# Later float32r copies in MLP 1's last block, and another low-word shift in MLP 2's weight conversions

## The chip, the cores and the metric

The kernel runs on one core of a Trainium2 chip. The metric is the device time of one execution in microseconds; lower is better. The kernel before takes 602.6 us (median of 3 runs, 602.4 to 602.93). Engines are called by their short names in the rows: PE is TensorE (PEld its weight loads), DVE VectorE, ACT ScalarE, POOL GpSimd, SP SyncE, whose queue issues most DMAs.

## The reference

The inputs pass through a blocked linear attention and two MLPs, each of 1536 tokens by 512 features with 2048 hidden features:

```python
x = attn(q, k, v, lam)                    # 2 batches, 8 heads, 768 tokens, 64 features a head
h = x @ w1_in                             # MLP 1
x = (h * np.clip(h + 3, 0, 6) / 6) @ w1_out
h = x @ w2_in                             # MLP 2
P = a[0] + a[1]*h + a[2]*h**2 + a[3]*h**3
Q = 1 + abs(b[0])*abs(h) + abs(b[1])*h**2
out = (P / (Q + 1e-6)) @ w2_out
```

The weights arrive as 64-bit floats. The kernel reads them as pairs of 32-bit words and makes each float32 value on the chip.

## The kernel before

**Tiling.** Tokens go in three blocks of 512, hidden features in 16 tiles of 128. One step `s` is one token block with one feature tile: steps 0 to 47 are MLP 1, steps 48 to 95 MLP 2. Each step has a first product `mm1(s)` (12 matmuls into `hb[s % 2]`, one of two PSUM banks), an activation, and a second product `mm2(s)` (12 matmuls into the four `acc` banks). Each operand is split into a high and a low float32r part, so a product takes three matmuls. `mm2` runs two to three steps behind `mm1`; the list `turns` fixes the order of the two on TensorE.

**Order.** The body runs under a manual schedule: every engine carries out its instructions in the order in which the program writes them, and waits by semaphores for the others. Tiles from a pool with `bufs=2` alternate between two buffers.

**Activation of MLP 2** (`act2`, lines 283 to 297, and `act2_rest`, 301 to 306). ScalarE writes |b0 h| into the PSUM bank `X` (L289), then h squared into `ta` (L290), `tb` (L291), `tc` (L292) and `td` (L293); L293 is the last reader of `hb`. VectorE adds `X` to `tb` (L294). GpSimd multiplies and adds (L295, L296). One step later in the program VectorE takes the reciprocal into the PSUM bank `Y` (L304) and multiplies (L305). `act_fin` then makes the high part `gh` on ScalarE (L280) and the low part `gl` on GpSimd (L281), which `mm2` reads.

**Weight conversion.** A job is one or two tiles of weights, loaded as raw 64-bit words. `conv_c` copies the scaled high words (ACT L153) and clamps them (DVE L154). `conv_l` or `conv_s` shifts them by three bits and brings in the top bits of the low words; `conv_l` uses a PSUM bank for that (X or Y), `conv_s` the raw tile. `conv_w` puts the sign in (DVE L194). `conv_h` makes the float32r copy on ScalarE (L207) and the low part on GpSimd (L208). In MLP 1's last block (steps 32 to 47) each step converts one tile of MLP 2's input weights and one of its output weights. The last three output tiles are converted in MLP 2: the list `later` holds their pieces, and each step from 52 on takes one piece off it, between `act_fin(s - 2)` and `mm1(s)` in program order.

**The places that the diff touches.** `pending` holds copies (`conv_h`) that are made in the next step, right behind that step's activation; before, only output weights go there. `late` selects, in `conv_s`, a form on VectorE alone (L181 and L184).

Of the kernel before, what the change touches and what calls it, by code (L numbers as in the profile page):

```python
# [10 lines left out]
U32 = mybir.dt.uint32  # L11
BF16 = mybir.dt.bfloat16
AF = mybir.ActivationFunctionType
ALU = mybir.AluOpType
# [16 lines left out]
def fused_kernel(  # L31
# [14 lines left out]
    nc = tc.nc  # L46
# [4 lines left out]
    KD = DM // 128  # L51
# [18 lines left out]
    X = ps.tile([128, 512], F32, name="X")  # L70
    Y = ps.tile([128, 512], F32, name="Y")
# [27 lines left out]
    jobs = [[(0, 0)], [(0, 1)]] + [[(0, f + 2)] * (f < NF - 2) + [(1, f)] for f in range(NF)]  # L99
    NJ1 = len(jobs)  # L100
    jobs += [[(2, p)] * (p < NF) + [(3, p - LAG)] * (p >= LAG) for p in range(NF + LAG)]
    N1 = NB * NF
# [5 lines left out]
    for s in range(NSTEP):  # L108
# [5 lines left out]
        while at < to:  # L114
            d, i = quarters[at]
# [3 lines left out]
    while at < len(quarters) - 8:  # L119
        d, i = quarters[at]  # L120
# [4 lines left out]
    def load_job(j):  # L125
        if j >= len(jobs):
            return
        t = []
        for m, f in jobs[j]:
            r = rp.tile([128, KD, 128, 2], U32, name=f"raw{m % 2}")  # L130
            if m % 2 == 0:
                nc.sync.dma_start(
                    r.rearrange("p k f t -> p k (f t)"),
                    w32[m].rearrange("(k p) f -> p k f", p=128)[:, :, 256 * f : 256 * f + 256],
                )
            else:
                nc.sync.dma_start(r.rearrange("p k f t -> p (k f t)"), w32[m][128 * f : 128 * f + 128, :])
            t.append(r)
        raw[j] = t

    conv = {}
# [12 lines left out]
        nc.vector.tensor_scalar(out=x, in0=x, scalar1=CMAX, scalar2=-CMAX, op0=ALU.min, op1=ALU.max)  # L154
        conv[j, i] = x

    def conv_l(j, i):

        if i >= len(jobs[j]):
            return  # L160
        x = conv[j, i]
        y = (X, Y)[i].bitcast(U32).rearrange("p (a b) -> p a b", a=KD)
        nc.scalar.activation(y, raw[j][i][:, :, :, 0], AF.Copy, scale=LOWS, bias=LOWB)
        nc.vector.scalar_tensor_tensor(  # L164
            out=y, in0=x.bitcast(U32), scalar=3, in1=y, op0=ALU.logical_shift_left, op1=ALU.bitwise_or
        )
        conv[j, i] = x, y, x.bitcast(U32)

    def conv_s(j, i, late=False):

        if i >= len(jobs[j]):
            return
        x = conv[j, i]
        y, r = x.bitcast(U32), raw[j][i]
        if not late:
            nc.scalar.activation(r[:, :, :, 0], r[:, :, :, 0], AF.Copy, scale=LOWS, bias=LOWB)
            nc.vector.scalar_tensor_tensor(
                out=y, in0=y, scalar=3, in1=r[:, :, :, 0], op0=ALU.logical_shift_left, op1=ALU.bitwise_or
            )
        else:  # L180
            nc.vector.tensor_scalar(  # L181
                out=y, in0=y, scalar1=3, scalar2=1, op0=ALU.logical_shift_left, op1=ALU.bitwise_or
            )
            nc.vector.scalar_tensor_tensor(  # L184
                out=y, in0=r[:, :, :, 0], scalar=29, in1=y, op0=ALU.logical_shift_right, op1=ALU.bitwise_or
            )
        conv[j, i] = x, y, r[:, :, :, 1]

    def conv_w(j, i):
# [21 lines left out]
    def mm1(s):  # L211
        tb, f = (s // NF) % NB, s % NF
        ih, il = W["in", f]
        h = hb[s % 2]
        for kk in range(KD):
            nc.tensor.matmul(h, lhsT=ih[:, kk, :], rhs=xh[tb][:, kk, :], start=kk == 0, stop=False)  # L216
        for kk in range(KD):
            nc.tensor.matmul(h, lhsT=il[:, kk, :], rhs=xh[tb][:, kk, :], start=False, stop=False)  # L218
        for kk in range(KD):
            nc.tensor.matmul(h, lhsT=ih[:, kk, :], rhs=xl[tb][:, kk, :], start=False, stop=kk == KD - 1)  # L220

    def mm2(s, ds=(0, 1, 2, 3)):
        tb, f = (s // NF) % NB, s % NF
        oh, ol = W["out", f]
        gh, gl = g_t[s]
        first = s < NB * NF
        st, sp = f == 0, f == NF - 1
        for d in ds:
            c = slice(128 * d, 128 * d + 128)
            if first:  # L230
                ops = ((oh[:, c], gh), (ol[:, c], gh), (oh[:, c], gl))
            else:
                ops = ((gh[:, c], oh), (gh[:, c], ol), (gl[:, c], oh))
            for i, (l, r) in enumerate(ops):
                nc.tensor.matmul(acc[d], lhsT=l, rhs=r, start=st and i == 0, stop=sp and i == 2)  # L235
            if sp:
                if first:
                    nc.scalar.activation(xh[tb][:, d, :], acc[d], AF.Copy, scale=1.0 / 6.0)
                    nc.vector.scalar_tensor_tensor(
                        out=xl[tb][:, d, :], in0=acc[d], scalar=1.0 / 6.0,  # L240
                        in1=xh[tb][:, d, :].bitcast(F32), op0=ALU.mult, op1=ALU.subtract,
                    )
                else:
                    o = rp.tile([128, KD, 128, 2], U32, name=f"raw{d % 2}").bitcast(F32)
                    o = o.rearrange("p k f t -> p (k f t)")[:, 0:DM]
                    row = TB * tb + 128 * d
                    if s == NSTEP - 1 and d == 3:
                        for e, eng, dma in ((0, nc.scalar.copy, nc.scalar), (1, nc.vector.tensor_copy, nc.sync)):
                            hf = slice(DM // 2 * e, DM // 2 * e + DM // 2)
                            eng(o[:, hf], acc[d][:, hf])  # L250
                            dma.dma_start(out[row : row + 128, hf], o[:, hf])
                    else:
                        nc.scalar.copy(o, acc[d])  # L253
                        nc.sync.dma_start(out[row : row + 128, :], o)
# [54 lines left out]
    with ExitStack() as actx:  # L309
# [106 lines left out]
        with tc.manual_schedule():  # L416
# [18 lines left out]
            for h2 in range(2):  # L435
                r = slice(64 * h2, 64 * h2 + 64)
                nc.vector.tensor_copy(lamq[r, :], lamb.rearrange("p (a b) -> p a b", b=2)[r, :, h2])
            for p in range(NP):
                nc.vector.tensor_tensor_scan(
                    out=qtab[:, p, :], data0=lamq[:, p : p + 1].to_broadcast([128, CH]), data1=zero,  # L440
                    initial=1.0, op0=ALU.mult, op1=ALU.add)
                for h2 in range(2):
                    hd = 2 * p + h2
                    nc.vector.tensor_tensor_scan(
                        out=dmat[:, h2, p, :], data0=lamb[:, hd : hd + 1].to_broadcast([128, CH]), data1=ident,
# [23 lines left out]
            att_t(2, hb)  # L469
            conv_all(conv_c, 0)  # L470
            conv_all(conv_s, 0)
            conv_all(conv_w, 0)
            att_o(1)
# [35 lines left out]
            for s in range(att_steps):  # L509
                c = CPT + s  # L510
                j = s + 3
# [41 lines left out]
    W2AT = N1 - NF  # L553
    with tc.manual_schedule():
        pending, later = [], []
        nc.scalar.activation(b1a, b_sb[:, 1:2], AF.Abs)
        todo = turns[turns.index((1, att_steps + 1)) :]
        for at, (kind, s, *qs) in enumerate(todo):
            if kind == 2:
                mm2(s, *qs)  # L560
                continue
            j = None
            if s + 2 < NJ1:
                j = s + 2
            elif s >= W2AT and s - W2AT + NJ1 < len(jobs):
                j = s - W2AT + NJ1
            if s == W2AT - 1:
                load_job(NJ1)
            if j is not None and j != NJ1 - 1:
                load_job(j + 1)  # L570
            n = 0 if j is None else len(jobs[j])
            if s < N1:
                mm1(s)
                act1(s)
                if todo[at + 1][0] == 2 and todo[at + 1][1] % NF == NF - 1:
                    act_fin(s)
                    mm2(*todo.pop(at + 1)[1:])
                for p in pending:
                    conv_h(*p)
                if n:  # L580
                    conv_c(j, 0)
                    conv_l(j, 0)
                    conv_w(j, 0)
                act_fin(s)
                if s == N1 - 1:

                    later += [(conv_c, j, 1, True), (conv_s, j, 1, True), (conv_w, j, 1), (conv_h, j, 1)]
                    n = 1
                if n > 1:
                    conv_c(j, 1)  # L590
                    conv_l(j, 1)
                    conv_w(j, 1)
            else:
                act2_rest(s - 1)
                act_fin(s - 2)
                if s > N1 + LAG2 and later:
                    f, *args = later.pop(0)
                    f(*args)
                mm1(s)
                act2(s)  # L600
                for p in pending:
                    conv_h(*p)
                if n:
                    later += [(conv_c, j, 0, True), (conv_s, j, 0, True), (conv_w, j, 0), (conv_h, j, 0)]
                n = 0
            pending = []
            for i in range(n):
                if jobs[j][i][0] % 2:
                    pending.append((j, i))
                else:  # L610
                    conv_h(j, i)
            if s == NSTEP - 1:
                act2_rest(s)
                act_fin(s - 1)
                act_fin(s)
# [29 lines left out]
```

## Time and profile before

| what | value |
|---|---|
| median of 3 runs | 602.6 us |
| profiled execution | 602.82 us |
| span of the profiled execution, first to last instruction | 600.9 us |
| TensorE busy | 588.1 us (98%) |
| VectorE busy | 445.2 us (74%) |
| ScalarE busy | 384.0 us (64%) |
| GpSimd busy | 366.8 us (61%) |
| granted TensorE clock | 1.00 of full speed |

Times within the profile count from the first instruction. The 1.9 us between the profiled execution's time and its span lie around the program's own instructions. Busy shares are averages over the whole span and don't tell which engine the others wait for in a given stretch.

### The profile page before, as it was taken

Reading aid. Unit: us, or ns where it says so; the run is one execution under the profiler, and the core shown is the slowest. Engines: PE = TensorE matmul, PEld = TensorE weight load, DVE = VectorE, ACT = ScalarE, POOL = GpSimd, SP = SyncE. Lnnn points to the kernel's source line nnn. Section 1 sums busy time; section 2 is a strip of 40 time slices with the busy share of each in tenths; the row PEclk is TensorE's granted clock in tenths of the full one; section 3 lists DMA queues with packets and bytes.
Section 4 is the critical chain, followed back from the end, with each engine's and each line's share of the span. In section 5 each row is a group of like instructions: output and inputs, shape, how many; then the busy total and the mean of one; then the engine's idle time right before and its main releaser. Section 6 shows DMA issues by size and latency. Waiting matters only on the chain.

```text
span 600.9 us, 8288 instructions
## 1 busy us (share of the span) xinstructions
PE 588.1 (98%) x3035; PEld 480.6 (80%) x3035; DVE 445.2 (74%) x476; ACT 384.0 (64%) x635; POOL 366.8 (61%) x291
## 2 busy tenths in 40 slices
PE   8898999999999999999999999999999999999997
PEld 5786888888888888888888787877788888888886
DVE  5877888787411011488888899999999888999991
ACT  2566465677422222588787877787887767877771
POOL 3756677566421222266676677688776677777772
PEclk9999999999999999999999999999999999999999
DMA  8987755364000000266655000000010000100001
GB/s 169 267 214 196 173 157 160 130 211 150 1 1 0 1 0 1 88 206 197 184 171 172 1 1 35 1 0 2 28 43 0 2 0 2 69 2 0 1 1 71
DMA packets 61289, 46.68 MB, mean 78 GB/s; under 512 B 39104, under 2 KB 55744, under 8 KB 61248
## 3 DMA queue, kind: packets, MB, share of 16 engines
q1 hardware_dynamic: 60960, 46.02, 26.9%
q8 instruction: 24, 0.39, 0.3%
q10 hardware_dynamic: 288, 0.14, 0.1%
q14 instruction: 17, 0.14, 0.1%
HBM read 43.00 MB, written 3.15 MB: 77 GB/s over the span
## 4 chain that ended last, share of the span: by engine, by line
PE 52%; DVE 24%; ACT 4%; issue 3%; POOL 1%; DVEq 0%; ACTq 0%
PE acc L235 26%; DVE Y L304 8%; PE hb L216 8%; PE hb L220 8%; PE hb L218 8%; DVE ta L154 2%; DVE X L164 2%; DVE ta L194 2%; DVE Y L164 2%; DVE tb L294 2%; DVE tb L194 2%; ACT ta L153 1%; DVE td L305 1%; DVE tb L154 1%; DVE raw L184 1%
## 5 line engine op out<-in xcount | busy, mean ns | idle before, releaser
L304 DVE RECIPROCAL Y<-tb 128x512 f32<-128x512 f32 x48 | 161.3, 3360 | 1.6
L281 POOL TENSOR_TENSOR gl<-td,gh 128x512 fp32r<-128x512 f32 x84 | 111.2, 1324 | 77.1 <-ACT gh L280 76.0
L216 PE MATMUL hb<-xh,wih 128*128 128x512 f32 x384 | 104.3, 393 | 0.5 <-ACT td L293 0.4
L218 PE MATMUL hb<-xh,wil 128*128 128x512 f32 x384 | 102.7, 389 | 0.0
L220 PE MATMUL hb<-xl,wih 128*128 128x512 f32 x384 | 102.6, 389 | 0.0
L295 POOL TENSOR_TENSOR tc<-ta,tc 128x512 f32<-128x512 f32 x48 | 62.2, 1295 | 58.2 <-ACT tc L292 58.2
L271 DVE SCALAR_TENSOR_TENSOR td<-tc,hb 128x512 f32<-128x512 f32 x48 | 32.8, 683 | 84.3 <-ACT tc L268 84.3
L216 PEld LDWEIGHTS hb<-xh,wih 128*128 128x128 f32 x384 | 71.1, 188 | 17.4 <-ACT td L293 1.8
L218 PEld LDWEIGHTS hb<-xh,wil 128*128 128x128 f32 x384 | 72.1, 188 | 15.2
L220 PEld LDWEIGHTS hb<-xl,wih 128*128 128x128 f32 x384 | 72.1, 188 | 15.0
L268 ACT ACTIVATE tc<-hb,c 128x512 f32<-128x512 f32 x48 | 32.9, 686 | 71.7 <-PE hb L220 71.6
L235 PE MATMUL acc<-gh,woh 128*128 128x512 f32 x192 | 76.1, 396 | 0.0
L235 PE MATMUL acc<-gl,woh 128*128 128x512 f32 x192 | 74.8, 390 | 0.0
L235 PE MATMUL acc<-gh,wol 128*128 128x512 f32 x192 | 74.8, 389 | 0.0
L280 ACT CAST gh<-td 128x512 fp32r<-128x512 f32 x84 | 52.0, 619 | 25.9 <-DVE td L271 13.8
L296 POOL TENSOR_TENSOR td<-td,tc 128x512 f32<-128x512 f32 x48 | 63.8, 1330 | 3.8
L208 POOL TENSOR_TENSOR wil<-ta,wih 128x512 fp32r<-128x512 f32 x32 | 41.4, 1294 | 34.7 <-ACT wih L207 34.7
L289 ACT ACTIVATE X<-hb,b_sb 128x512 f32<-128x512 f32 x48 | 31.8, 662 | 42.8 <-PE hb L220 34.1
L235 PE MATMUL acc<-woh,gl 128*128 128x512 f32 x144 | 56.5, 392 | 1.1 <-POOL gl L281 1.1
L235 PE MATMUL acc<-woh,gh 128*128 128x512 f32 x144 | 56.2, 390 | 0.3 <-ACT raw L253 0.3
L235 PE MATMUL acc<-wol,gh 128*128 128x512 f32 x144 | 56.0, 389 | 0.0
L208 POOL TENSOR_TENSOR wol<-tb,woh 128x512 fp32r<-128x512 f32 x29 | 38.4, 1324 | 14.4 <-ACT woh L207 14.4
(104 smaller groups left out, 1029.1 us busy)
## 6 DMA issues: line engine op xcount, KB each, us to landing
raw<-in_moe_w_in_dram SPq DMA_DIRECT2D x32, 512.0 KB, 3.8
raw<-in_moe_w_out_dram SPq DMA_DIRECT2D x32, 512.0 KB, 4.6
qn<-in_q_dram SPq DMA_DIRECT2D x12, 256.0 KB, 5.5
kn<-in_k_dram SPq DMA_DIRECT2D x12, 256.0 KB, 5.3
vn<-in_v_dram SPq DMA_DIRECT2D x12, 256.0 KB, 4.8
out_dram<-raw SPq DMA_DIRECT2D x11, 256.0 KB, 2.2
out_dram<-raw ACTq DMA_DIRECT2D x1, 128.0 KB, 1.8
out_dram<-raw SPq DMA_DIRECT2D x1, 128.0 KB, 1.7
```

The lines of the kernel that those rows point to most:

```text
L208: nc.gpsimd.tensor_tensor(lo, x, hi.bitcast(F32), op=ALU.subtract)
L216: nc.tensor.matmul(h, lhsT=ih[:, kk, :], rhs=xh[tb][:, kk, :], start=kk == 0, stop=False)
L218: nc.tensor.matmul(h, lhsT=il[:, kk, :], rhs=xh[tb][:, kk, :], start=False, stop=False)
L220: nc.tensor.matmul(h, lhsT=ih[:, kk, :], rhs=xl[tb][:, kk, :], start=False, stop=kk == KD - 1)
L235: nc.tensor.matmul(acc[d], lhsT=l, rhs=r, start=st and i == 0, stop=sp and i == 2)
L268: nc.scalar.activation(t, h, AF.Relu, bias=c3)
L271: nc.vector.scalar_tensor_tensor(out=g, in0=t, scalar=6.0, in1=h, op0=ALU.min, op1=ALU.mult)
L280: nc.scalar.copy(gh, g)
L281: nc.gpsimd.tensor_tensor(gl, g, gh.bitcast(F32), op=ALU.subtract)
L295: nc.gpsimd.tensor_tensor(b1, h2, b1, op=ALU.mult)
L296: nc.gpsimd.tensor_tensor(a1, a1, b1, op=ALU.add)
L304: nc.vector.reciprocal(Y, q1)
```

## The change

It has three parts.

- In MLP 1's last block the float32r copies of MLP 2's input weights go into `pending` as well, so they are made in the next step.
- The last input tile's low words go into bank `Y` in place of `X`.
- A late job has new pieces. The low words are shifted on ScalarE, in place in the raw tile, as in the attention stage; VectorE merges them in two halves, one step each; the sign (`conv_w`) and the float32r copy (`conv_h`) are then taken in one step. Before, the four pieces were `conv_c`, `conv_s`, `conv_w` and `conv_h`.

```diff
-    def conv_l(j, i):
+    def conv_l(j, i, bank=None):
...
-        y = (X, Y)[i].bitcast(U32).rearrange("p (a b) -> p a b", a=KD)
+        y = (bank or (X, Y)[i]).bitcast(U32).rearrange("p (a b) -> p a b", a=KD)
...
-    def conv_s(j, i, late=False):
+    def conv_s(j, i, half=None):
...
-        x = conv[j, i]
+        x = conv[j, i][0] if half else conv[j, i]
         y, r = x.bitcast(U32), raw[j][i]
-        if not late:
+        if not half:
             nc.scalar.activation(r[:, :, :, 0], r[:, :, :, 0], AF.Copy, scale=LOWS, bias=LOWB)
-            nc.vector.scalar_tensor_tensor(
-                out=y, in0=y, scalar=3, in1=r[:, :, :, 0], op0=ALU.logical_shift_left, op1=ALU.bitwise_or
-            )
-        else:
-            nc.vector.tensor_scalar(
-                out=y, in0=y, scalar1=3, scalar2=1, op0=ALU.logical_shift_left, op1=ALU.bitwise_or
-            )
-            nc.vector.scalar_tensor_tensor(
-                out=y, in0=r[:, :, :, 0], scalar=29, in1=y, op0=ALU.logical_shift_right, op1=ALU.bitwise_or
-            )
+        k = slice(0, KD) if half is None else slice(KD // 2 * half, KD // 2 * half + KD // 2)
+        nc.vector.scalar_tensor_tensor(
+            out=y[:, k], in0=y[:, k], scalar=3, in1=r[:, k, :, 0], op0=ALU.logical_shift_left, op1=ALU.bitwise_or
+        )
         conv[j, i] = x, y, r[:, :, :, 1]
...
+        def late_job(j, i):
+            return [((conv_c, j, i, True),), ((conv_s, j, i, 0),), ((conv_s, j, i, 1),), ((conv_w, j, i), (conv_h, j, i))]
...
-                    conv_l(j, 0)
+                    conv_l(j, 0, Y if s == N1 - 1 else None)
...
-                    later += [(conv_c, j, 1, True), (conv_s, j, 1, True), (conv_w, j, 1), (conv_h, j, 1)]
+                    later += late_job(j, 1)
...
-                    f, *args = later.pop(0)
-                    f(*args)
+                    for f, *args in later.pop(0):
+                        f(*args)
...
-                    later += [(conv_c, j, 0, True), (conv_s, j, 0, True), (conv_w, j, 0), (conv_h, j, 0)]
+                    later += late_job(j, 0)
...
-                if jobs[j][i][0] % 2:
+                if jobs[j][i][0]:
+
                     pending.append((j, i))
```

## Rows read from the trace of the kernel before

**Rows 1.** The page, parts 1 and 6: TensorE's busy time; one kind of load.

```profile
PE 588.1 (98%) x3035; PEld 480.6 (80%) x3035; DVE 445.2 (74%) x476; ACT 384.0 (64%) x635; POOL 366.8 (61%) x291
...
raw<-in_moe_w_out_dram SPq DMA_DIRECT2D x32, 512.0 KB, 4.6
```

**Rows 2.** Windows: stretch, length, busy (count) of PE, PEld, DVE, ACT, POOL; PEclk; DMA.

```profile
130.00:333.00 203.00, 203.00 (x897) 168.11 (x896) 105.22 (x155) 110.41 (x192) 95.29 (x74) 1.00 0.30 91
```

**Rows 3.** Timeline, TensorE, 340 to 369 us: start, us, instruction, [idle before <-releaser].

```profile
340.36 1.20 PE L216 MATMUL hb<-xh,wih 128*128 128x512 f32 x4 [0.37 <-ACT td L293]
...
352.03 1.07 PE L216 MATMUL hb<-xh,wih 128*128 128x512 f32 x4
...
357.47 1.07 PE L216 MATMUL hb<-xh,wih 128*128 128x512 f32 x4
...
368.63 0.76 PEld L216 LDWEIGHTS hb<-xh,wih 128*128 128x128 f32 x4 [0.54 <-ACT td L293]
```

**Rows 4.** The chain that ended last, in order of time, 425 to 445 us.

```profile
436.76 0.91 PE hb L216 x4
```

**Rows 5.** Timeline, VectorE, 357 to 370 us.

```profile
357.62 0.68 DVE L294 TENSOR_TENSOR tb<-tb,X 128x512 f32<-128x512 f32 x1
...
358.33 3.36 DVE L304 RECIPROCAL Y<-tb 128x512 f32<-128x512 f32 x1
...
361.80 0.69 DVE L305 TENSOR_TENSOR td<-td,Y 128x512 f32<-128x512 f32 x1
...
362.40 0.42 DVE L181 TENSOR_SCALAR raw<-raw 128x512 uint32<-128x512 uint32 x1
...
362.86 1.67 DVE L184 SCALAR_TENSOR_TENSOR raw<-raw,raw 128x512 uint32<-128x512 uint32 x1
...
369.23 0.69 DVE L194 SCALAR_TENSOR_TENSOR raw<-raw,raw 128x512 uint32<-128x512 uint32 x1
```

**Rows 6.** Timeline, ScalarE, 358 to 371 us.

```profile
358.40 0.66 ACT L289 ACTIVATE X<-hb,b_sb 128x512 f32<-128x512 f32 x1 [0.72 <-DVE tb L294]
...
365.22 0.66 ACT L289 ACTIVATE X<-hb,b_sb 128x512 f32<-128x512 f32 x1 [2.08 <-DVE tb L294]
...
366.43 0.82 ACT L291 ACTIVATE tb<-ta,cq,b1a 128x512 f32<-128x512 f32 x1
...
367.82 0.76 ACT L293 ACTIVATE td<-hb,a_sb 128x512 f32<-128x512 f32 x1
...
369.95 0.62 ACT L207 CAST woh<-raw 128x512 fp32r<-128x512 f32 x1
370.61 0.66 ACT L289 ACTIVATE X<-hb,b_sb 128x512 f32<-128x512 f32 x1
```

**Rows 7.** Source views of L176 and L177: durations in ns, least/median/most.

```profile
L176 ACT ACTIVATE raw<-raw x20: 661/679/696, 17.0 to 111.8; 128x512 uint32<-128x512 uint32 x20
...
L177 DVE SCALAR_TENSOR_TENSOR ta<-ta,raw x11: 677/1529/1762, 17.7 to 113.6; 128x512 uint32<-128x512 uint32 x11
```

**Rows 8.** Timeline, GpSimd, 362 to 364 us.

```profile
362.54 1.44 POOL L296 TENSOR_TENSOR td<-td,tc 128x512 f32<-128x512 f32 x1
```

**Rows 9.** Timeline, ScalarE and GpSimd at the change from MLP 1 to MLP 2.

```profile
330.68 0.61 ACT L280 CAST gh<-td 128x512 fp32r<-128x512 f32 x1
...
332.88 0.62 ACT L207 CAST wih<-ta 128x512 fp32r<-128x512 f32 x1 [1.58 <-DVE ta L194]
...
335.33 0.76 ACT L292 ACTIVATE tc<-hb,a_sb 128x512 f32<-128x512 f32 x1
...
336.17 1.29 POOL L295 TENSOR_TENSOR tc<-ta,tc 128x512 f32<-128x512 f32 x1 [1.30 <-ACT tc L292]
...
337.22 0.60 ACT L290 ACTIVATE ta<-hb 128x512 f32<-128x512 f32 x1
337.54 1.29 POOL L296 TENSOR_TENSOR td<-td,tc 128x512 f32<-128x512 f32 x1
...
338.86 0.78 ACT L292 ACTIVATE tc<-hb,a_sb 128x512 f32<-128x512 f32 x1 [0.19 <-POOL td L296]
339.54 0.77 ACT L293 ACTIVATE td<-hb,a_sb 128x512 f32<-128x512 f32 x1
```

## The prediction

> **What bounds the kernel now.** I read the page first: TensorE is busy 588.1 of 600.9 us [rows 1]. The windows view then says where it is not. From 130 to 333 us, the body of MLP 1, it is busy 203.00 of 203.00 us at a granted clock of 1.00 [rows 2]: nothing that an edit there takes off another engine shortens that stretch. So only the stretch after 333 us can give time back, and every wait newly put on TensorE there is paid in full.
>
> TensorE's timeline after 333 us shows where it waits. One mm1 and one mm2 are 24 matmuls and take 5.44 us (352.03 to 357.47). mm1(51) at 340.36 idles for L293, the last reader of its hb bank, and mm1(56) at 368.63 waits for the same line [rows 3]. From mm1(53) at 352.03 to mm1(68) at 436.76 [rows 4] are 15 steps: 84.73 us where 15 x 5.44 = 81.6 would do. About 3.1 us are lost in this stretch, and they are all that the new low-word shift can win.
>
> VectorE's timeline tells why. Its ring in MLP 2 is L294(s), reciprocal, L305(s), the late conversion op if there is one, L294(s+1). The steps are 0.71 us (357.62 to 358.33), 3.47 (to 361.80) and 0.60 (to 362.40): 4.78 without a late op, under TensorE's 5.44. The old shift puts in 0.42 and 1.67 us, the mask 0.69 [rows 5]. Four steps with one late job exceed TensorE's four.
>
> ScalarE's timeline shows the coupling that matters. L289(s) overwrites the X bank that L294(s-1) reads, so L289 at 365.22 starts right behind it after 2.08 us of idling. Four activations later L293 frees hb for TensorE [rows 6].
>
> **The change, part by part.** To count steps: late jobs are taken from step 52 on; L294 at 357.62 belongs to step 52, L289 at 365.22 to 54 and at 370.61 to 55.
>
> *The shift.* Removed per job: 0.42 and 1.67 us on VectorE. Added: one ScalarE pass over the low words, and two half operations with both inputs in SBUF. The ScalarE pass is bounded by the same form in the attention stage, 661 to 696 ns [rows 7]. It stands ahead of L289(53), where ScalarE idled 0.72 us [rows 6]; that idle covers it. Without the cover it would add 0.7 us per job. For a half, the floor is half of the 677 ns full operation, 0.34, and the ceiling is the whole 0.68. I take 0.42, as L181, the nearest short operation in that very place, plus 0.04 of turnaround: 0.46 (362.40 to 362.86) [rows 5].
>
> A port wait can come on top: L184, right behind L181, took 1.67 us while GpSimd's L296 ran from 362.54 to 363.98 [rows 5, 8]; the full operation ranged from 677 to 1762 ns in the attention stage [rows 7]. The first operation behind L305 had no such wait [rows 5], so I give a half none in the first job. In jobs two and three I allow one half 0.43 (worked out below).
>
> The Trainium skill speaks against halves here. Its page "SBUF — State Buffer", section "SBUF: two separate sides", says that a VectorE operation with two SBUF inputs and a GpSimd operation exclude each other for a whole instruction. By it a half could wait as the whole did, twice per job; by the row of the first operation it need not. The first reading is a rival below, with its own time.
>
> *The last entry of the late job.* This decides. Before, the sign mask (DVE L194) and the float32r copy (ACT L207) are taken in successive steps. L207 of step 55 came at 369.95, 0.72 after the mask of step 54 began at 369.23, without a wait [rows 5, 6]. Now the third step is used for the second half, and mask and copy are taken in one step. On ScalarE the copy of step s stands ahead of L289(s). On VectorE the mask of step s stands behind L305(s-1), so behind the reciprocal of s-1. ScalarE therefore can't start L289(s) just behind L294(s-1): it waits for the reciprocal and the mask too. What is queued behind the copy is L289 to L293 of that step, and TensorE's mm1(s+2) waits for L293.
>
> In before's clock: L294(54) = 357.62 + 2 x (4.78 + 0.46) = 368.10. Mask at 368.10 + 4.78 = 372.88, copy 0.72 later, L289(55) 0.66 after that (369.95 to 370.61): 374.26, in place of right behind L294(54) at 368.1. From L289 to TensorE's restart are 3.41 us (365.22, over L293 at 367.82, to 368.63) [rows 3, 6]: mm1(57) at 377.67. Unstalled it is due at 352.03 + 4 x 5.44 = 373.79. **TensorE waits 3.9 us for job one.** The cover that is gone is the lag: TensorE would not wait if L294(54) came by 364.2.
>
> Jobs two and three. L291(55) ends 2.03 after L289(55) (365.22 to 366.43, plus 0.82) and L294(55) follows at 374.26 + 2.05 = 376.31, that is 1.36 before mm1(57). Three steps with short late ops, 3 x 5.24, and the one port wait bring L294(58) to 14.79 after mm1(57). That wait: by then L289 is paced by the copy in place of X, so L295 reaches into the half by about half a microsecond; between 0 and the 0.99 that L184 lost (1.67 - 0.68) I take 0.43. The chain from L294 to mm1 is 4.78 + 0.72 + 0.66 + 3.41 = 9.57, so mm1(61) can start at 24.36; due is 4 x 5.44 = 21.76, plus 0.25 for the restart and a short gl wait. **Each waits 2.35 us.** The three waits are 8.6 us, and the restart and gl terms 0.25 each, 0.75 (the matmul group after a wait takes 1.20 instead of 1.07 [rows 3]).
>
> *Copies that wait a step in MLP 1's last block.* 16 copies (0.62 us on ScalarE, about 1.29 on GpSimd, each) move behind the next step's L268. TensorE never waits in that stage, so 15 of them are worth nothing [rows 2]; if that cover failed, a 0.62 us copy per step would be the price. They issue no DMA. The last one crosses into MLP 2: it leaves ScalarE's place at 332.88, where ScalarE had idled for the mask, and goes behind act2(48). The Y bank lets L289(48) start without waiting for the X bank, right behind L280: 330.68 + 0.61 = 331.3. But its GpSimd half now stands behind L295(48) and L296(48). L292(48) follows 1.92 later (L289 to L293 is 2.60 [rows 6], less the 0.68 from 338.86 to 339.54) at 333.2, L295 0.84 after it, L296 1.37 after that at 335.4; the subtraction, at 1.29 each, runs from 336.7 to 338.0. L290(49) writes the ta buffer that this subtraction reads (two buffers alternate), so it moves from 337.22 to 338.0. From L290 to L293 were 2.32, with 0.19 of L292 waiting for L296 that falls away: 2.1, so L293(49) comes at 340.1 in place of 339.54 [rows 9]. **mm1(51) comes 0.5 us later**, and all behind it. If the subtraction held nothing up, the wait at 340.36 and the gl wait after it would go instead: about 1.3 us less than before, 1.8 less than my sum.
>
> *DMA.* A raw buffer is released one step later because the mask is; the 512 KB load into it lands in about 4.6 us [rows 1], and five steps (27 us) lie before it is read. Nothing, unless SyncE's queue fell more than 20 us behind.
>
> **Sum.** Profiled 602.8 (span 600.9 and 1.9 around it) + 0.5 + 8.6 + 0.75 - 3.1 = 609.6. The median of the runs is 0.2 lower: 609.4, rounded to 609.5, about 1.1% slower.
>
> **Rivals.** (1) *Faster.* The copy's wait falls into slack that TensorE has, and only the cheaper shift counts: 602.6 + 0.5 - 3.1 = 600.0. It decides if L294(54) comes by 364.2, 3.9 us before my 368.1. For it: VectorE gains 0.2 us a step on TensorE at 5.24. Against: four steps of that are under 1 us.
> (2) *Only the first wait.* TensorE's own 3.9 us stop lets VectorE catch up for good: 609.5 - 2 x 2.6 = 604.3. For it: L294(55) then lies 1.36 before mm1(57). Against: the 9.57 us chain recurs and three steps win only 0.6.
> (3) *The port.* All six halves wait as L184 did: 6 x 0.99 - 2 x 0.43 = 5.1 more, 614.6. Against: the first operation behind L305 was free of it [rows 5].
> (4) *The clock.* A stop of 3.9 us lets the granted clock fall to the lower level; one mm1 at half speed costs 2.72 more: 612.2. The granted clock was 1.00 through MLP 1 [rows 2], with no idling so long. The Trainium skill's "TensorE: Matmul & The Clock Gate", Part 1, says that an idle TensorE is put to half its clock; no row of this kernel shows it.
>
> **How the numbers follow.** My sum 0.74, its own range 607 to 612 (down 1.8 for the change-over and some for halves at 0.34 without waits; up 2.1 if one half per job loses 0.99). Rival 1 0.08, rival 2 0.08, rival 3 0.07, rival 4 0.03. I predict 609.5. The range takes in rival 2 and rival 4 and part of 3: 604.5 to 613. About 0.2% is what a measurement can tell here: faster 0.08; same 0.03 (the low edge of rival 2); slower 0.89.
>
> **What would show it.** Right: three TensorE waits for L293, about 22 to 25 us apart, the first near 374 and 4 us long, the others over 2; before each, ACT L207 idle some 5 us for DVE's mask; no L184-like 1.67 us row; L290 near 338 idle for POOL. L289 directly behind X with no such idle proves the central step wrong. So would a TensorE without waits after 370, or a mask that runs ahead of the reciprocal.

## The result, and the profile after

The changed kernel takes 606.81 us (median of 4 runs, 606.42 to 607.04) against 602.59 us: 1.0069 times as long, 95% interval 1.0051 to 1.0086. The forecast was slower, 609.5 us in a range of 604.5 to 613. Its profiled execution took 606.79 us with a span of 604.8. One execution each of two variants below, start_one_earlier and same_buffer, took far longer than the rest (981 and 1189 us) and is left out of their ratios.

The diff shortens the functions ahead of the MLPs, so lines move up: L294 of before is L288, L304 is L298, L305 is L299, L289 is L283, L293 is L287, L207 is L201, L216 is L210 and L194 is L188.

The page's busy times, part 1, answer to [rows 1]:

```profile
PE 587.1 (97%) x3035; PEld 480.5 (79%) x3035; DVE 443.0 (73%) x476; ACT 383.1 (63%) x638; POOL 364.0 (60%) x291
```

Every engine is busy for less time than before, TensorE and VectorE too, and the span is 3.9 us longer: busy time was not added, waiting was. The windows view puts a bound on where (columns as in [rows 2]):

```profile
130.00:333.00 203.00, 203.00 (x897) 168.11 (x896) 105.73 (x155) 110.13 (x193) 94.85 (x74) 1.00 0.29 91
333.00:370.00 37.00, 37.00 (x164) 30.43 (x164) 35.65 (x28) 29.00 (x46) 27.47 (x22) 1.00 0.00 1
370.00:434.00 64.00, 57.05 (x248) 45.72 (x247) 54.64 (x43) 47.30 (x75) 45.42 (x36) 1.00 0.03 9
```

TensorE now works without a gap until 370 us, across the change from MLP 1 to MLP 2 as well, and then loses 7 of 64 us. Its timeline there (beside [rows 3]) has three rows with a wait; the rows of mm1(53) and mm1(58), without one, are used further down:

```profile
350.63 1.07 PE L210 MATMUL hb<-xh,wih 128*128 128x512 f32 x4
...
375.76 1.19 PE L210 MATMUL hb<-xh,wih 128*128 128x512 f32 x4 [3.22 <-ACT td L287]
...
381.47 1.07 PE L210 MATMUL hb<-xh,wih 128*128 128x512 f32 x4
...
399.83 1.20 PE L210 MATMUL hb<-xh,wih 128*128 128x512 f32 x4 [1.88 <-ACT td L287]
...
423.88 1.19 PE L210 MATMUL hb<-xh,wih 128*128 128x512 f32 x4 [1.86 <-ACT td L287]
```

The three with a wait are mm1(57), mm1(61) and mm1(65), 24 us apart, and each waits for ScalarE to free its hb bank. What ScalarE was doing is in its own timeline (compare [rows 6]):

```profile
366.11 0.62 ACT L274 CAST gh<-td 128x512 fp32r<-128x512 f32 x1 [0.76 <-DVE td L299]
371.83 0.62 ACT L201 CAST woh<-raw 128x512 fp32r<-128x512 f32 x1 [5.10 <-DVE raw L188]
372.36 0.66 ACT L283 ACTIVATE X<-hb,b_sb 128x512 f32<-128x512 f32 x1
...
374.95 0.77 ACT L287 ACTIVATE td<-hb,a_sb 128x512 f32<-128x512 f32 x1
```

ScalarE stands 5.10 us in front of the float32r copy until VectorE has made the sign mask (L188). VectorE's timeline shows why that takes so long (compare [rows 5]; its first two rows are a half of the shift and what follows it):

```profile
360.87 0.42 DVE L178 SCALAR_TENSOR_TENSOR raw<-raw,raw 128x256 uint32<-128x256 uint32 x1
361.21 0.68 DVE L288 TENSOR_TENSOR tb<-tb,X 128x512 f32<-128x512 f32 x1
...
366.33 0.68 DVE L288 TENSOR_TENSOR tb<-tb,X 128x512 f32<-128x512 f32 x1
367.05 3.36 DVE L298 RECIPROCAL Y<-tb 128x512 f32<-128x512 f32 x1
370.51 0.69 DVE L299 TENSOR_TENSOR td<-td,Y 128x512 f32<-128x512 f32 x1
371.12 0.68 DVE L188 SCALAR_TENSOR_TENSOR raw<-raw,raw 128x512 uint32<-128x512 uint32 x1
374.41 0.69 DVE L288 TENSOR_TENSOR tb<-tb,X 128x512 f32<-128x512 f32 x1 [2.61 <-ACT tb L285]
```

The mask has its turn behind the 3.36 us reciprocal. The last row is the other side of the same knot: VectorE now idles 2.61 us for ScalarE, which was held by VectorE.

At the change from MLP 1 to MLP 2 the timeline of ScalarE and GpSimd (compare [rows 9]) reads:

```profile
331.75 0.65 ACT L283 ACTIVATE X<-hb,b_sb 128x512 f32<-128x512 f32 x1
...
336.08 0.60 ACT L284 ACTIVATE ta<-hb 128x512 f32<-128x512 f32 x1
...
337.12 1.30 POOL L202 TENSOR_TENSOR wil<-ta,wih 128x512 fp32r<-128x512 f32 x1
...
338.11 0.77 ACT L287 ACTIVATE td<-hb,a_sb 128x512 f32<-128x512 f32 x1
```

L284 writes its ta buffer at 336.08, a microsecond before the subtraction that I had it wait for even begins. So the two use different buffers, and L287 comes at 338.11 in place of 339.54. TensorE's rows for mm1(50), a wait for gl and mm1(52) of the kernel before, and for mm1(50) to mm1(52) of the changed kernel:

```profile
337.11 1.07 PE L216 MATMUL hb<-xh,wih 128*128 128x512 f32 x4
...
344.18 0.50 PE L235 MATMUL acc<-woh,gl 128*128 128x512 f32 x1 [0.35 <-POOL gl L281]
...
346.59 1.07 PE L216 MATMUL hb<-xh,wih 128*128 128x512 f32 x4
```

```profile
336.89 1.07 PE L210 MATMUL hb<-xh,wih 128*128 128x512 f32 x4
...
339.61 1.07 PE L210 MATMUL hb<-xh,wih 128*128 128x512 f32 x4
...
345.18 1.07 PE L210 MATMUL hb<-xh,wih 128*128 128x512 f32 x4
```

Before, these two steps took 9.5 us, with a wait at mm1(51) [rows 3] and the one for gl; now they take 8.3 us and have no wait.

### The profile page after: what moved, and what is told of

Same layout as the page of the kernel before. It is cut to its first block, busy times and chain, and to the rows that moved or that the text cites. A ratio compares the mean times of both kernels' runs of the same rounds, so it can differ in the third digit from the quotient of the medians.

```text
span 604.8 us, 8289 instructions
## 1 busy us (share of the span) xinstructions
PE 587.1 (97%) x3035; PEld 480.5 (79%) x3035; DVE 443.0 (73%) x476; ACT 383.1 (63%) x638; POOL 364.0 (60%) x291
## 4 chain that ended last, share of the span: by engine, by line
PE 54%; DVE 22%; ACT 5%; issue 3%; DVEq 0%; ACTq 0%
PE acc L229 27%; PE hb L210 9%; PE hb L212 9%; PE hb L214 9%; DVE Y L298 8%; DVE ta L154 2%; ACT ta L153 2%; DVE X L164 2%; DVE ta L188 2%; DVE Y L164 2%; DVE tb L188 1%; DVE tb L288 1%; DVE td L299 1%; DVE tb L154 1%; ACT tb L285 1%
## 5 line engine op out<-in xcount | busy, mean ns | idle before, releaser
L298 DVE RECIPROCAL Y<-tb 128x512 f32<-128x512 f32 x48 | 161.3, 3361 | 1.6
L275 POOL TENSOR_TENSOR gl<-td,gh 128x512 fp32r<-128x512 f32 x84 | 110.0, 1309 | 78.0 <-ACT gh L274 77.3
L210 PE MATMUL hb<-xh,wih 128*128 128x512 f32 x384 | 104.2, 393 | 7.0 <-ACT td L287 7.0
L289 POOL TENSOR_TENSOR tc<-ta,tc 128x512 f32<-128x512 f32 x48 | 62.3, 1298 | 53.7 <-ACT tc L286 53.6
L210 PEld LDWEIGHTS hb<-xh,wih 128*128 128x128 f32 x384 | 71.1, 188 | 23.9 <-ACT td L287 8.2
L229 PE MATMUL acc<-gh,woh 128*128 128x512 f32 x192 | 76.1, 396 | 0.0
L229 PE MATMUL acc<-gl,woh 128*128 128x512 f32 x192 | 74.9, 390 | 0.0
L229 PE MATMUL acc<-gh,wol 128*128 128x512 f32 x192 | 74.8, 390 | 0.0
L290 POOL TENSOR_TENSOR td<-td,tc 128x512 f32<-128x512 f32 x48 | 62.7, 1306 | 3.8
L202 POOL TENSOR_TENSOR wil<-ta,wih 128x512 fp32r<-128x512 f32 x32 | 41.4, 1293 | 33.8 <-ACT wih L201 33.8
L229 PE MATMUL acc<-woh,gl 128*128 128x512 f32 x144 | 56.4, 392 | 0.0
L283 ACT ACTIVATE X<-hb,b_sb 128x512 f32<-128x512 f32 x48 | 31.8, 662 | 38.4 <-PE hb L214 35.9
L229 PE MATMUL acc<-woh,gh 128*128 128x512 f32 x144 | 56.1, 389 | 0.0
L229 PE MATMUL acc<-wol,gh 128*128 128x512 f32 x144 | 56.0, 389 | 0.0
L202 POOL TENSOR_TENSOR wol<-tb,woh 128x512 fp32r<-128x512 f32 x29 | 38.4, 1323 | 14.0 <-ACT woh L201 14.0
```

Source lines behind the costliest of these rows:

```text
L202: nc.gpsimd.tensor_tensor(lo, x, hi.bitcast(F32), op=ALU.subtract)
L275: nc.gpsimd.tensor_tensor(gl, g, gh.bitcast(F32), op=ALU.subtract)
L289: nc.gpsimd.tensor_tensor(b1, h2, b1, op=ALU.mult)
L290: nc.gpsimd.tensor_tensor(a1, a1, b1, op=ALU.add)
L298: nc.vector.reciprocal(Y, q1)
```

## The experiments

All times are medians beside runs of the kernel before on the same chip (602.6 to 603.0 us). Diffs are against the changed kernel where nothing else is said.

**mask_with_half.** The mask moves to the step of the second half.

```diff
-((conv_s, j, i, 1),), ((conv_w, j, i), (conv_h, j, i))]
+((conv_s, j, i, 1), (conv_w, j, i)), ((conv_h, j, i),)]
```

> The changed kernel with the sign mask taken in the step of the second half, so that the float32r copy has the fourth step for itself. Theory A (ScalarE stands behind a mask that VectorE makes only after the reciprocal of the step before): the copy finds its mask made a step earlier, the three idle stretches of ScalarE of 5.1 us and the three TensorE waits of 3.2, 1.9 and 1.9 us go, VectorE's four steps take 4 x 4.78 + 0.7 + 0.35 + 0.35 + 0.6 = 21.1 us under TensorE's 21.8, and the time is 606.8 - 8.1 = 598.7 us (598.3 to 599.6). Theory B (the added ScalarE pass and the two halves themselves hold the ring up): the same operations run, so the time stays at 606 to 607 us.

Measured: 600.59 us, ratio 0.9964 (0.9951 to 0.9977). The 5.1 us waits of ScalarE are gone, and theory B with them: the added operations cost no 8 us. But it is 2 us short of theory A's number. VectorE's and GpSimd's timelines name the rest:

```profile
366.11 0.42 DVE L178 SCALAR_TENSOR_TENSOR raw<-raw,raw 128x256 uint32<-128x256 uint32 x1
366.56 1.67 DVE L188 SCALAR_TENSOR_TENSOR raw<-raw,raw 128x512 uint32<-128x512 uint32 x1
```

```profile
366.24 1.44 POOL L290 TENSOR_TENSOR td<-td,tc 128x512 f32<-128x512 f32 x1
367.64 1.74 POOL L275 TENSOR_TENSOR gl<-td,gh 128x512 fp32r<-128x512 f32 x1
```

The half gets in before GpSimd's L290 and costs 0.42 us. The mask right behind it takes 1.67 us where it took 0.68 in the changed kernel, and ends 0.55 us behind L290, which ends at 367.68. This is the same 1.67 us as the old L184 in [rows 5], with another operation in its place: what is slow is the place right behind another late operation, not the shift. The Trainium skill's page "SBUF — State Buffer", section "SBUF: two separate sides", says so of VectorE operations with two SBUF inputs: one of the two engines holds the port for a whole instruction. The trace agrees: 0.99 us are added, and the next GpSimd operation, L275, is stretched to 1.74 in turn. It comes once per late job, and TensorE takes 83.7 us from mm1(53) to mm1(68) in place of 81.6: these are the 2 us.

**mask_before_recip.** Mask and copy stay in one step, but the mask is written ahead of the reciprocal.

```diff
+                piece = later.pop(0) if s > N1 + LAG2 and later else ()
+                for f, *args in piece:
+                    if f is conv_w:
+                        f(*args)
                 act2_rest(s - 1)
                 act_fin(s - 2)
-                if s > N1 + LAG2 and later:
-                    for f, *args in later.pop(0):
+                for f, *args in piece:
+                    if f is not conv_w:
                         f(*args)
```

> The changed kernel with mask and copy still in one step, but the mask written ahead of the reciprocal, so that it comes right behind L288 of the step before. Theory A: ScalarE waits for one 0.7 us operation and not for 0.7 + 3.5 + 0.6 + 0.7 us; its wait at the copy falls from 5.1 us to under 1.5, TensorE does not wait, 598.7 us (598.3 to 600.0). Theory A2 (a mask and a copy in one step hold ScalarE up wherever they stand): three TensorE waits stay, 605 to 607 us.

Measured: 599.11 us, ratio 0.9939 (0.9924 to 0.9954). ScalarE's wait at the copy:

```profile
368.54 0.62 ACT L201 CAST woh<-raw 128x512 fp32r<-128x512 f32 x1 [1.42 <-DVE raw L188]
```

It falls from 5.10 to 1.42 us, and TensorE is busy for 89.00 of 89.00 us between 345 and 434 us. A mask and a copy in one step cost TensorE nothing here; the reciprocal ahead of the mask does. This is the run that decides for theory A over A2.

**start_two_later** and **start_one_earlier.** When the late pieces begin.

```diff
-                if s > N1 + LAG2 and later:
+                if s > N1 + LAG2 + 2 and later:     # start_one_earlier: N1 + LAG2 - 1
```

> The changed kernel with the late pieces taken from step 54 on in place of 52. Theory A with the lag: TensorE's wait is the lag of VectorE less about 4.1 us, and two more steps without a late operation take 2 x (5.44 - 4.78) = 1.3 us off the lag before the first wait; the first wait falls from 3.2 to about 1.9 us, the other two, which start from the state that the wait before leaves, stay at 1.9: 606.8 - 1.3 = 605.5 us. Rival (each wait is a fixed price of the 5.1 us that ScalarE stands): three waits as before, 606.8 us.

> The changed kernel with the late pieces taken from step 51 on in place of 52. Theory A with the lag: VectorE has one free step fewer to catch up before the first copy, its lag there is 0.66 us larger and so is TensorE's first wait (3.2 to 3.9 us idle); the other two stay at 1.9: 607.4 us. Rival (a fixed price of ScalarE's 5.1 us): 3.2 and 606.8 us.

Measured: 607.91 us, ratio 1.009 (1.0073 to 1.0107), and 609.17 us (median of three), ratio 1.0099 (1.0068 to 1.013). As totals both missed. The first wait, which is what was to be told apart, did follow the lag. TensorE's timelines of start_two_later and of start_one_earlier:

```profile
385.72 1.34 PE L210 MATMUL hb<-xh,wih 128*128 128x512 f32 x4 [1.95 <-ACT td L287]
386.87 1.91 PE L212 MATMUL hb<-xh,wil 128*128 128x512 f32 x4
```

```profile
371.28 1.35 PE L210 MATMUL hb<-xh,wih 128*128 128x512 f32 x4 [3.69 <-ACT td L287]
372.43 1.91 PE L212 MATMUL hb<-xh,wil 128*128 128x512 f32 x4
```

ScalarE stands 5.1 us each time in all three kernels, yet TensorE waits 3.69, 3.22 and 1.95 us: 0.47 more with one free step less, 1.27 less with two free steps more (0.66 and 1.3 were expected). So the wait is VectorE's lag less what TensorE can run ahead, and not a fixed price. The totals missed for two reasons. In start_two_later the last tile came too late for its own product: TensorE's waits view lists 1.3 us at L229 for L201's copy, 0.9 us for L202's subtraction and 1.0 us for the output copy (L247) behind them. And in both, the second row above shows four matmuls taking 1.91 us where they take 1.07: the granted clock had halved (last section).

**first_part_only.** The kernel before with the copies that wait a step and bank Y alone.

```diff
-                    conv_l(j, 0)                                 # against the kernel before
+                    conv_l(j, 0, Y if s == N1 - 1 else None)
...
-                if jobs[j][i][0] % 2:
+                if jobs[j][i][0]:
```

> The kernel before with the first two parts alone: the input weights' copies wait a step, and the last tile uses bank Y; the late shift stays as it was. My prediction's step (the squared h of step 49 has to wait for a buffer that the last subtraction reads): mm1(51) comes 0.5 us later, 603.1 us. Rival, which the changed kernel's trace speaks for (no such wait, both the hb wait and the gl wait behind it go): 1.3 us less, 601.3 us. Third: the copies move nothing that ends last, 602.6 us.

Measured: 601.91 us, ratio 0.9987 (0.9978 to 0.9996). TensorE waits neither at mm1(51) nor for the gl behind it; the later waits of before are all there. My step predicted 603.1 and is wrong. The gain measured, 0.1% with an interval of the same size, is below what left the trace: from mm1(50) to mm1(68) its profiled execution takes 98.2 us and the kernel before 99.5, 1.3 us less. That execution reached mm1(50) 1.2 us later than the kernel before (338.34 against 337.11), with a granted clock of 0.99 in the first 130 us, ahead of all that the edit touches. Executions ranged from 601.0 to 603.3; the two at a mean granted clock of 1.0 took 601.0 and 601.5.

**copy_own_step** and **whole_shift.** Five pieces from step 51, each its own step; and four pieces with the low words merged in one operation.

```diff
+            return [((conv_c, j, i, True),), ((conv_s, j, i, 0),), ((conv_s, j, i, 1),), ((conv_w, j, i),), ((conv_h, j, i),)]
-                if s > N1 + LAG2 and later:
+                if s > N1 + LAG2 - 1 and later:
...
+            return [((conv_c, j, i, True),), ((conv_s, j, i),), ((conv_w, j, i),), ((conv_h, j, i),)]     # whole_shift
```

> The changed kernel with five pieces per late job, so that mask and copy have a step each and the halves too; the pieces start one step earlier (51) so that the last copy still comes before its product. Theory A: no wait of 5.1 us on ScalarE, no operation on VectorE behind another late one, so no 1.67 us port wait like that of the run with the mask behind the second half: 599 us (598.5 to 599.8), as with the mask ahead of the reciprocal. Rival (the gain of that run came from moving the mask out from behind the multiply, not from freeing ScalarE): about 602 us or more.

> The changed kernel with the low words merged in one operation in place of two halves; copy in a step of its own, four pieces as before. The halves matter only if the whole operation meets GpSimd at the shared port. Theory: the first late operation behind the multiply gets the port between two GpSimd operations, takes 0.7 us, VectorE's four steps stay under TensorE's: 599 us. Rival (a whole operation waits about 1 us, as the old second shift operation did): four steps take about 22 us, TensorE waits some tenths per job again, 600 to 601 us.

Measured: 598.98 us, ratio 0.9934 (0.9917 to 0.9952), and 598.64 us, ratio 0.993 (0.9915 to 0.9946). In neither does ScalarE wait at a late copy. In whole_shift VectorE's timeline has the merge and the mask in successive steps, both first behind the multiply and both unhindered:

```profile
361.64 0.69 DVE L178 SCALAR_TENSOR_TENSOR raw<-raw,raw 128x512 uint32<-128x512 uint32 x1
...
367.03 0.68 DVE L188 SCALAR_TENSOR_TENSOR raw<-raw,raw 128x512 uint32<-128x512 uint32 x1
```

Halving was not needed. It was what filled the third step and pushed mask and copy together. With the shift on ScalarE, a whole merge and the old four steps, TensorE is busy for 101.00 of the 101.00 us from 333 to 434:

```profile
333.00:345.00 12.00, 12.00 (x54) 9.81 (x53) 11.32 (x11) 11.90 (x21) 8.89 (x8) 1.00 0.00 1
345.00:434.00 89.00, 89.00 (x394) 73.67 (x393) 86.53 (x63) 74.02 (x116) 71.92 (x55) 1.00 0.05 18
```

The intervals of whole_shift, copy_own_step and mask_before_recip overlap; all three beat the kernel before, and which is best is not settled.

**late_part_only**, **shift_alone** and **bank_x.** Taking the first two parts out again, from the changed kernel (late_part_only) and from whole_shift (shift_alone); bank_x takes only bank Y out of whole_shift.

```diff
-                    conv_l(j, 0, Y if s == N1 - 1 else None)     # all three
+                    conv_l(j, 0)
...
-                if jobs[j][i][0]:                                # not in bank_x
+                if jobs[j][i][0] % 2:
```

> The changed kernel without its first two parts: copies of the input weights at once, as before, the last tile in bank X; the late job as changed. If the parts add up, the waits of 0.6 and 0.6 us at the start of MLP 2 come back on top of the three long ones: 606.8 + 1.3 = 608.1 us. Rival (the earlier start is eaten by the next wait, since a TensorE that starts later leaves VectorE time to catch up): 606.8 us.

> The run whole_shift without the first two parts (copies at once, bank X): the new shift alone, in its best form. It should lose the two waits at the start of MLP 2, 0.65 us at mm1(51) and 0.6 us for gl, that the kernel before has too: 598.6 + 1.3 = 599.9 us; against the kernel before a gain of 2.7 us from the shift. Rival (the early start and the shift gain the same microsecond): 598.6 to 599 us.

> The run whole_shift with the last input tile in bank X, as before the change; the copies still wait a step. If bank Y is what lets MLP 2's first activation start early, L283 of step 48 waits for the sign mask that reads X, until 333.4 in place of 331.75 us, and TensorE waits about 1.0 us at mm1(51) and 0.5 us for gl: 600.2 us. If the copy that moved out of ScalarE's way is enough by itself: 598.6 us.

Measured: 610.12 us, ratio 1.0123 (1.0103 to 1.0144); 599.38 us, ratio 0.9947 (0.9931 to 0.9964); 599.95 us, ratio 0.9961 (0.9948 to 0.9974). The two short waits come back in late_part_only (0.38 us at mm1(51), 0.36 us for gl), and mm1(50) to mm1(52) take 9.5 us again, 1.2 more than in the changed kernel: the parts add up there. Behind its first long wait, of 3.35 us, the granted clock is 0.53 from 377 to 380 us, and the next wait is 0.43 us in place of 1.88, which gives back what the clock had cost (1.4 us). So its profiled execution of 608.01 us is 1.2 us over the changed kernel's. The other three, which have no trace, took 609.4 to 610.8 us at mean granted clocks of 0.988 to 0.994.

In shift_alone the same two waits are back (0.34 and 0.34 us), and mm1(50) to mm1(52) take 1.2 us more than in whole_shift; its median is only 0.7 us higher, between the 599.9 expected and the rival's 599. In bank_x ScalarE's L283 idles 1.64 us for the mask that reads X, and TensorE waits 0.76 and 0.35 us, more than in shift_alone: the later copies without bank Y are worth less than nothing, 10.0 us from mm1(50) to mm1(52) against 9.5. Bank Y is what makes that part pay. Bank Y without the later copies was not run.

**same_buffer** and **same_buffer_trace.** One kernel, whole_shift with step 49 writing into the buffer that the last subtraction reads.

```diff
-        h2 = tp.tile([128, TB], F32, name="ta")
+        h2 = same.pop(s) if s in same else tp.tile([128, TB], F32, name="ta")
...
                 for p in pending:
+                    same[s + 1] = conv[p][0].rearrange("p a b -> p (a b)")
                     conv_h(*p)
```

> The run whole_shift with one edit: step 49 writes its squared h into the very buffer that the last input tile's subtraction reads, as my prediction had assumed. If the assumption about the buffer was the only wrong link of that step, L284 of step 49 now idles for GpSimd's subtraction (it ends near 338.4 us, so L284 moves from 336.1 to 338.5), TensorE waits about 1.7 us at mm1(51) and some 0.5 us for gl behind it, and the time is 598.6 + 2.4 = 601.0 us. If the chain behind it was wrong too (slack before mm1(51)), it stays within 0.5 us of whole_shift.

> The kernel of same_buffer once more, for its trace, since the execution that was profiled there did not run at the usual rate. If the time of 601.0 us comes from the buffer, L286 of step 49 (the line that was L284) idles some 2 us for GpSimd's subtraction near 338.4 us, and TensorE idles about 1.7 us at mm1(51) and 0.5 us for gl. If TensorE shows no wait there, the 2.3 us lie elsewhere.

Measured: 600.97 us, ratio 0.9973 (0.9963 to 0.9982), and 601.16 us with the trace. ScalarE's and TensorE's timelines (the edit adds lines, so L284 is L286 and L287 is L289):

```profile
338.92 0.60 ACT L286 ACTIVATE ta<-hb 128x512 f32<-128x512 f32 x1 [2.29 <-POOL wil L202]
```

```profile
337.36 1.07 PE L210 MATMUL hb<-xh,wih 128*128 128x512 f32 x4
...
341.75 1.21 PE L210 MATMUL hb<-xh,wih 128*128 128x512 f32 x4 [1.52 <-ACT td L289]
...
345.57 0.50 PE L229 MATMUL acc<-woh,gl 128*128 128x512 f32 x1 [0.31 <-POOL gl L275]
...
347.97 1.07 PE L210 MATMUL hb<-xh,wih 128*128 128x512 f32 x4
```

The wait that I had predicted appears once the buffer is forced to be that one, and costs what this run's expectation said: 2.3 us over whole_shift. Against the kernel before, mm1(50) to mm1(52) take 10.6 us in place of 9.5, so the change-over then costs 1.1 us and not the 0.5 of the prediction.

## Why the prediction was right, and where it was off

- *The mask and the copy in one step.* Right in mechanism and in place: three waits for L287 at mm1(57), mm1(61) and mm1(65), ScalarE idle 5.1 us before each, VectorE's mask behind the reciprocal. mask_before_recip shows the cause: moving the mask ahead of the reciprocal removes all three.
- *The size of the three waits.* This is the mis-sized term: 3.9, 2.35 and 2.35 us were predicted, 8.6 in all. mm1(57) came 375.76 - (350.63 + 4 x 5.44) = 3.4 us late (mm1(53) starts at 350.63), mm1(61) 399.83 - (381.47 + 3 x 5.44) = 2.0 us (mm1(58) at 381.47), mm1(65) likewise 2.0: 7.4 in all, 1.2 less. A half with its turnaround takes 0.34 us (360.87 to 361.21) and not 0.46, and the copy is followed by L283 after 0.53 us (371.83 to 372.36) and not 0.66; for the first wait, with two halves, that is 0.37 of the 0.5. The restart and gl term, 0.25 a wait, was right: mm1(57) to mm1(58) take 5.71 us, 0.27 over 5.44.
- *The port wait of one half in jobs two and three.* Right in kind. The source view of the changed kernel's halves, L178 (least/median/most in ns):

```profile
L178 DVE SCALAR_TENSOR_TENSOR raw<-raw,raw x6: 420/420/1035, 360.9 to 414.1; 128x256 uint32<-128x256 uint32 x6
```

  Most take 0.42 us, as assumed. One half in each of jobs two and three took longer, 1.03 us at 384.32 and 1.02 at 408.39: 0.6 us more, where I had allowed 0.43. GpSimd's L289, the prediction's L295, runs beside the first of them from 383.78 to 385.08, as it said.
- *The gain from the cheaper shift, 3.1 us.* Right: no wait for gl or for the output copy is listed between 333 and 445 us in the changed kernel. shift_alone, which has the shift as one whole operation with mask and copy in steps of their own, takes 81.6 us from mm1(53) to mm1(68) (351.66 to 433.26), the figure of the prediction (before it was 84.6, with mm1(68) at 436.60 in TensorE's timeline, 0.16 ahead of the chain's row), and beats the kernel before by 0.5%, 3.2 us.
- *The copies of MLP 1's last block.* Right: TensorE is still busy for 203.00 of 203.00 us from 130 to 333 us, so 15 of the 16 are worth nothing.
- *The change-over.* This step failed. The prediction let L290 of step 49 wait for the last tile's subtraction because "two buffers alternate". In the trace it writes at 336.08 and the subtraction runs from 337.12: the program had put it into the other buffer. The sentence that two buffers alternate, which stands in the part on the kernel before too, doesn't hold at this place. In place of 0.5 us lost, the two waits at the start of MLP 2 are gone: from mm1(50) to mm1(52) are 8.3 us (336.89 to 345.18) and not 9.5 (337.11 to 346.59), 1.2 us won. same_buffer shows that the chain behind the assumption was right in kind; its size was not, 1.1 us where 0.5 was predicted, since the gh copy ahead of L283(48) came at 331.23 and not at 330.68, and the subtraction with it later. The 1.7 us that this makes are near the 1.8 that the prediction named as its lower case, and most of the 2.7 us between 609.5 and 606.8; the smaller waits are the rest.
- *The ranges.* The sum's own range was 607 to 612 us, and 606.8 lies just below it: its two wrong terms erred to the same side. The stated range of 604.5 to 613 holds the result because it was widened for rivals 2 to 4.
- *The rivals.* Rival 1, slack that swallows the wait, and rival 2, the first wait only, are out by the three rows. Rival 3, all halves held at the port, is out by the source view of the halves above. Rival 4, the clock, did not occur in the changed kernel's profiled execution (granted 1.00 from 370 to 434 us), but it exists, as below. The other three executions have a mean granted clock of 0.997 and no trace, so whether it occurred there is open; they took no longer.

## What to carry to other kernels

When two pieces of work that depend on each other across engines are put into one slot of a software pipeline, look at what stands in front of the first in its own queue and behind the second in the other: here an in-order queue stood still for 5 us for one 0.7 us operation, and the cure was to move that operation ahead of the long one, or to give the two a step each. What a stop of an engine that feeds TensorE costs is how late the feeding engines are by then, less what TensorE can still run ahead, and not the length of the stop: the same 5.1 us made TensorE wait between 0.35 and 3.69 us. And whether a buffer conflicts is to be read from the program's own assignment; "two buffers alternate" was a guess.

## What the hardware showed that was not expected

TensorE's clock can fall to its lower level after such a wait. The windows view of start_one_earlier (columns as in [rows 2]):

```profile
365.00:372.40 7.40, 3.71 (x16) 2.73 (x15) 4.65 (x5) 5.01 (x9) 2.95 (x3) 0.98 0.21 71
372.40:375.70 3.30, 3.30 (x9) 2.61 (x8) 3.20 (x4) 3.27 (x6) 2.87 (x3) 0.52 0.00 0
375.70:390.00 14.30, 14.30 (x64) 11.80 (x63) 13.96 (x10) 8.71 (x14) 11.02 (x9) 1.00 0.00 1
```

After 3.69 us of idling, TensorE ran 3.30 us at a granted clock of 0.52, that is at 1.2 and not 2.4 GHz. The four matmuls at 372.43 above took 1.91 us, where four took 1.08 in the changed kernel. About 3.30 x (1 - 0.52) = 1.6 us are lost. The Trainium skill's "TensorE: Matmul & The Clock Gate", Part 1, says that an idle TensorE is put to half its clock, and here the trace agrees. But the length of the wait alone did not decide it: 1.95 us of idling brought it on in start_two_later (granted 0.57 from 387 to 390.5 us), and 3.22 us in the changed kernel's profiled execution did not. What else decides is open. Most of the cost was given back: the slow stretch lets VectorE catch up, and the next wait was 0.35 us in place of 1.88. In start_one_earlier the clock fell once more, behind the third wait, of 1.89 us (granted 0.53 from 421.0 to 423.5 us); no late job comes behind it that could give this back, and it is the larger part of the 2.4 us between its profiled execution (609.17 us) and the changed kernel's. That is why the two kernels' totals say little about the lag and their single waits say it well.
